# Block sums of the output weights: a table of their own over slots 25 to 56, laid back by DMA, and a new order of the steady batches

## The chip, the cores and the metric

One core of a Trainium2 chip runs the whole program. The metric is device time in microseconds (us); lower is better. Engine names are those of the profile: PE (TensorE matmul), PEld (TensorE weight loads), DVE (VectorE), ACT (ScalarE), POOL (GpSimd), SP (SyncE, which here issues nearly all DMAs).

## What is computed

The reference, cut to what matters: an attention over 32 learned memories, then a feed-forward layer with a hard-swish gate, all in fp32.

```python
# q, k, v: (8, 8, 576, 64)   phi: (8, 8, 576, 32)   w_in: (512, 2048)   w_out: (2048, 512)
a = softmax(phi, over the 32 memories)
k_m, v_m = einsum('bhsm,bhsd->bhmd', a, k), einsum('bhsm,bhsd->bhmd', a, v)
attn = softmax(q @ k_m.T / 8)
x = (attn @ v_m), heads side by side: (8 * 576, 512)
h = x @ w_in
out = (h * clip(h + 3, 0, 6) / 6) @ w_out
```

## The kernel before

**Tiling.** A batch has 576 tokens: two halves of 256 and 320 (the last 64 of a batch are a rest, joined in pairs over two batches). `v_m` is folded into `w_in` for each batch (`fold`, L424), so that the first product (`gemm1`) runs over 256 probabilities instead of 512 features. The 2048 hidden features are 16 tiles of 128. An fp32 product is made of three fp32r products: each operand is split into a rounded high part and the difference, the low part.

**First stages: slots.** Batches 0 to 2 run through 56 slots. A slot is one tile of 128 features for a whole batch: `g` (`gemm1`, 12 matmuls, L487), `u` (relu on ACT, L497), `m` (gate on DVE, L503), `k` (rest tokens, ACT), `h` (high part on ACT, L516), `l` (low part on DVE, L521), and two slots later (`LAG`) `a` (`gemm2`, L541). `BEGIN` is a hand-written order of slots 0 to 39 with the preparation of the weights and of the attention; `THIRD` is a table of what else is put into slots 40 to 55 (batch 2). From slot 8 on, one PSUM tile `ph` serves all slots, so the next `gemm1` must wait until the gate of the slot before has read it.

**Steady batches: units.** Batches 3 to 7 run in 32 steps each. Two steps make a unit, two tiles of 128 features, and the second product of a unit is done with Strassen's seven block products instead of eight (`products`, L685). It needs sums and differences of the four 256-column blocks of `w_out`: four blocks stay in `w2_sb` (two of them replaced by differences) and three sums per unit of weights are kept in DRAM (`streams`) and fetched again for each use (`stream<-kept`). `FOURTH`, `STEADY` and `EVERY` are the tables of what else is done in which step: `xa` and `xe` (subtract the maximum, exponential of phi), `mem` (the `pk` matmuls, L319), `sc` and `ct` (scores, L357, and their transposition on DVE, L373), `fo`, `vh`, `vl` (fold of `w_in` and its split), `fetch` (a chunk of `w_in` back from DRAM), `kv`, `pt`, `pn` (loads).

**The block sums before.** `tw` adds the high and low part of a unit's weights to whole fp32 numbers (POOL, L639), `ts` makes the three sums (POOL, L644, L645), `th` splits them (ACT L648, DVE L649, through `halve`) and stores them, `td` makes the two differences (POOL, L660) and `dd` splits these into `w2_sb` (ACT, DVE). Units 6, 7, 5, 0, 1, 2 and 3 are done in `THIRD`, 4 in `FOURTH`, and the differences of 5, 6 and 7 in steps 6 to 15 of batch 3 (`tl`, POOL L668, L670). Each engine runs its instructions in the written order.

Of the kernel before, what the change touches and what calls it, by code (L numbers as in the profile page):

```python
# [10 lines left out]
F32 = mybir.dt.float32  # L11
F32R = mybir.dt.float32r
# [9 lines left out]
P = 128  # L22
# [16 lines left out]
TMP = {"tag": "tmp", "bufs": 3}  # L39
# [69 lines left out]
5 xa.N.0 / 6 xe.N.0 xa.N.1 / 7 xe.N.1 xa.N.2 / 8 xe.N.2 mem.N / 9 nr.N nk.N q.N.0 pn.M / 10 q.N.1 / 11 tp.N tk.N  # L109
/ 12 sc.N.0 ct.N.0 / 13 cm.N.0 pt.M / 14 cs.N.0 sc.N.1 ct.N.1 fetch.N.0 / 15 cm.N.1 ex.N.0 kv.M.0 / 16 cs.N.1 ds.N.0 dr.N.0 kv.M.1  # L110
/ 17 ex.N.1 dm.N.0 kv.M.2 fetch.N.1
/ 20 fo.N.0 vh.N.0.0 vl.N.0.0 / 21 vh.N.0.1 vl.N.0.1 fetch.N.2 / 22 ds.N.1 dr.N.1 mx.M.0 kv.M.3 / 23 bt.N.0 dm.N.1
/ 24 fo.N.1 vh.N.1.0 vl.N.1.0 bh.N.0 / 25 vh.N.1.1 vl.N.1.1 bl.N.0 fetch.N.3 / 26 mx.M.1 kv.M.4 / 27 bt.N.1 mt.M mo.M
/ 28 fo.N.2 vh.N.2.0 vl.N.2.0 / 29 vh.N.2.1 vl.N.2.1 sp.M
"""


@with_exitstack
def attention_ffn_kernel(ctx: ExitStack, tc: tile.TileContext, pn, pt, kv, kl, qt, w1, w2, out):
# [16 lines left out]
    places, turns = {}, [0]  # L136
# [494 lines left out]
    def blocks_(u, half):
        return w2_sb[u][:, half].rearrange("p (x c) -> p x c", c=VC)

    def blocks(u, half):
        return blocks_(u, half).bitcast(F32)

    def sum_whole(u):
        staged[u] = sb.tile([P, 4, VC], F32, name="whole", **TMP)
        nc.gpsimd.tensor_tensor(staged[u], blocks(u, 0), blocks(u, 1), ALU.add)  # L639

    def sum_streams(u):
        w = staged[u]
        s_ = staged[u, "s"] = sb.tile([P, 3, VC], F32, name="sums", **O_RING)
        nc.gpsimd.tensor_tensor(s_[:, 1:3], w[:, 0:2], w[:, 2:4], ALU.add)  # L644
        nc.gpsimd.tensor_tensor(s_[:, 0], w[:, 0], w[:, 3], ALU.add)  # L645
# [5 lines left out]
    def keep_streams(u, k):  # L651
        xs = ((1, 2), (0,))[k]
        t = sb.tile([P, len(xs), 2, VC], F32R, name="parts", **TMP)
        halve(t[:, :, 0], t[:, :, 1], staged[u, "s"][:, xs[0] : xs[-1] + 1])
        for k, x in enumerate(xs):
            nc.sync.dma_start(out=streams[u][x], in_=t[:, k].bitcast(F32))

    def difference(u):
        w = staged[u]
        nc.gpsimd.tensor_tensor(w[:, 1:3], w[:, 1:3], w[:, 0::3], ALU.subtract)  # L660

    def late_difference(u, k):
        if k == 0:
            staged[u] = sb.tile([P, 4, VC], F32, name="whole", **O_RING)
        d = staged[u]
        if k < 2:
            part = blocks(u, k)
            nc.gpsimd.tensor_tensor(d[:, 0::3] if k else d[:, 1:3], part[:, 1:3], part[:, 0::3], ALU.subtract)  # L668
        else:
            nc.gpsimd.tensor_tensor(d[:, 1:3], d[:, 1:3], d[:, 0::3], ALU.add)  # L670
# [18 lines left out]
    BLOCK = {"A22": 0, "M7": 1, "M6": 2, "M1": 3, "M5": 4, "M2": 5, "A11": 6}  # L689

    def rounded_pair(low_ring):
        high = xpool.tile([P, 7, P], F32R, name="high", tag="probs00") if low_ring[0] % 2 == 0 else None
        if high is None:
            high = sb.tile([P, 7, P], F32R, name="high", **TMP)
        low_ring[0] += 1
        return high, sb.tile([P, 7, P], F32R, name="low", **TMP)

    ring = [0]

    class Unit:  # L700
# [61 lines left out]
        def products(self, part):  # L762
# [11 lines left out]
            todo = {
                0: (("A11", 0, 1, kept(2)), ("M5", 0, 0, kept(3)), ("M2", 1, 0, kept(0))),
                1: (("A22", 2, 0, kept(1)), ("M6", 3, 1, part and stream(1)), ("M7", 3, 0, part and stream(2)),
                    ("M1", 2, 1, part and stream(0))),
            }[part]
# [6 lines left out]
        def leave_first(self):  # L785
# [3 lines left out]
            nc.scalar.mul(self.x[:, 3], m[1][:, :VC], 1.0 / 6.0)  # L789

        def leave_second(self):
            m, x = sums[self.b, self.half], self.x
            o = sb.tile([P, 4, VC], F32, name="o", **O_RING)
            nc.scalar.mul(x[:, 1], m[2][:, :VC], 1.0 / 6.0)
            m1 = m[2][:, VC:].unsqueeze(1).broadcast_to([P, 2, VC])
# [3 lines left out]
            self.o = o  # L799
# [13 lines left out]
    class RestUnit:  # L813
# [4 lines left out]
        def total(self):  # L818
            own = {0: ("probs10", wpool), 2: ("probs00", xpool)}.get(self.u)
# [292 lines left out]
```

## Time and profile before

| | us |
|---|---|
| median of 3 runs (lowest, highest) | 723.74 (723.48, 724.48) |
| the profiled execution, its own time | 723.54 |
| its span in the trace | 721.8 |
| PE busy (weight loads apart) | 690.0, 96% of the span |
| DVE, ACT, POOL busy | 558.3, 387.1, 323.8 |

The span is what the rows below are counted in; 1.7 us of the execution lie outside it. A busy PE is not PE at its peak, since matmuls are pipelined and a matmul's length is longer than the distance to the next. Slots and units are found in the trace by their `gemm1`: slot 25 begins at 138.01, slot 40 at 202.62, the first unit at 293.11, its second `gemm1` at 302.48, the last step of batch 7 ends shortly after 702.

### The profile page before, as it was taken

Reading aid. Unit: us, or ns where it says so; the run is one execution under the profiler, and the core shown is the slowest. Engines: PE = TensorE matmul, PEld = TensorE weight load, DVE = VectorE, ACT = ScalarE, POOL = GpSimd, SP = SyncE. Lnnn points to the kernel's source line nnn. Section 1 sums busy time; section 2 is a strip of 40 time slices with the busy share of each in tenths; the row PEclk is TensorE's granted clock in tenths of the full one; section 3 lists DMA queues with packets and bytes.
Section 4 is the critical chain, followed back from the end, with each engine's and each line's share of the span. In section 5 each row is a group of like instructions: output and inputs, shape, how many; then the busy total and the mean of one; then the engine's idle time right before and its main releaser. Section 6 shows DMA issues by size and latency. Waiting matters only on the chain.

```text
span 721.8 us, 14655 instructions
## 1 busy us (share of the span) xinstructions
PE 690.0 (96%) x5618; PEld 584.5 (81%) x5622; DVE 558.3 (77%) x986; ACT 387.1 (54%) x786; POOL 323.8 (45%) x315
## 2 busy tenths in 40 slices
PE   8999999999999989799999999999999999999997
PEld 4456777888787766588889898888989989889997
DVE  4899986766366776688998779886898768977765
ACT  4677776544344445354655455554555546555553
POOL 1645331521227555358645345452646336444434
PEclk9999999999999999899999999999999999999999
DMA  9987671737143833569782398836983466736351
GB/s 360 416 332 272 227 276 57 273 112 250 51 149 125 316 154 110 175 223 343 257 308 77 103 349 298 308 119 223 345 308 114 132 231 214 277 107 210 133 182 45
DMA packets 56413, 154.46 MB, mean 214 GB/s; under 512 B 6168, under 2 KB 7192, under 8 KB 51736
## 3 DMA queue, kind: packets, MB, share of 16 engines
q1 hardware_dynamic: 56264, 153.47, 60.0%
q8 instruction: 44, 0.72, 0.4%
q14 instruction: 25, 0.20, 0.1%
q10 hardware_dynamic: 80, 0.07, 0.0%
HBM read 131.48 MB, written 22.03 MB: 213 GB/s over the span
## 4 chain that ended last, share of the span: by engine, by line
PE 67%; DVE 17%; ACT 6%; DMA 3%; issue 3%; POOL 2%; SPq 0%; ACTq 0%; DVEq 0%; POOLq 0%
PE acc L685 25%; PE acc L541 14%; PE ph L715 13%; PE ph L487 8%; PE pv L424 4%; DVE low L760 3%; DVE parts L649 2%; DMA stream<-kept 2%; PE acc L873 2%; DVE gf L503 2%; DVE gated L734 1%; DVE glo L521 1%; ACT high L755 1%; DVE gated L744 1%; DVE pnat L305 1%
## 5 line engine op out<-in xcount | busy, mean ns | idle before, releaser
L748 POOL TENSOR_TENSOR gated<-gated 128x256 f32<-128x256 f32 x80 | 77.3, 967 | 201.4 <-DVE gated L734 178.1
L760 DVE TENSOR_TENSOR low<-gated,high 128x384 fp32r<-128x384 f32 (+1 forms) x160 | 136.6, 855 | 27.4 <-ACT high L755 25.3
L715 PE MATMUL ph<-probs,both 128*128 128x256 f32 (+1 forms) x960 | 152.5, 294 | 1.7 <-DVE gf L503 1.7
L755 ACT CAST high<-gated 128x384 fp32r<-128x384 f32 (+1 forms) x160 | 90.6, 568 | 87.8 <-DVE gated L744 79.9
L715 PEld LDWEIGHTS ph<-probs,both 128*128 128x128 f32 x960 | 133.0, 188 | 2.5 <-DVE gf L503 2.2
L685 PE MATMUL acc<-w,high 128*128 128x256 f32 x640 | 123.9, 286 | 0.6 <-ACT high L755 0.3
L721 ACT ACTIVATE gf<-ph,three 128x256 f32<-128x256 f32 (+1 forms) x160 | 80.1, 500 | 64.5 <-PE ph L715 63.9
L685 PEld LDWEIGHTS acc<-w,high 128*128 128x128 f32 x640 | 99.4, 188 | 18.8 <-issue 6.3
L541 PE MATMUL acc<-w,ghi 128*128 128x512 f32 x384 | 101.9, 401 | 0.0
L734 DVE SCALAR_TENSOR_TENSOR gated<-gf,ph 128x256 f32<-128x256 f32 x160 | 65.7, 410 | 38.3 <-ACT gf L721 38.0
L685 PE MATMUL acc<-w,low 128*128 128x256 f32 x320 | 90.7, 283 | 2.2 <-DVE low L760 2.0
L685 PE MATMUL acc<-stream,high 128*128 128x256 f32 x480 | 89.1, 281 | 1.7 <-DMA stream<-kept 1.6
L541 PEld LDWEIGHTS acc<-w,ghi 128*128 128x128 f32 x384 | 70.1, 191 | 25.2 <-issue 5.7
L487 PEld LDWEIGHTS ph<-probs,both 128*128 128x128 f32 x528 | 74.0, 188 | 18.3 <-DVE gf L503 13.4
L487 PE MATMUL ph<-probs,both 128*128 128x256 f32 (+1 forms) x528 | 78.1, 297 | 8.3 <-DVE gf L503 8.2
L685 PEld LDWEIGHTS acc<-stream,high 128*128 128x128 f32 x480 | 73.3, 188 | 2.8 <-DMA stream<-kept 2.8
L685 PE MATMUL acc<-stream,low 128*128 128x256 f32 x240 | 67.2, 280 | 0.0
L685 PEld LDWEIGHTS acc<-w,low 128*128 128x128 f32 x320 | 60.2, 188 | 4.0 <-DVE low L760 3.8
L497 ACT ACTIVATE gf<-ph,three 128x576 f32<-128x576 f32 (+2 forms) x52 | 36.6, 705 | 43.4 <-PE ph L487 37.4
L503 DVE SCALAR_TENSOR_TENSOR gf<-gf,ph 128x576 f32<-128x576 f32 x44 | 32.9, 748 | 30.0 <-ACT gf L497 29.9
L541 PE MATMUL acc<-w,glo 128*128 128x512 f32 x192 | 53.8, 389 | 0.0
L444 DVE TENSOR_TENSOR both<-pv,both 128x512 fp32r<-128x512 f32 x62 | 42.3, 683 | 14.5 <-ACT both L435 14.3
(116 smaller groups left out, 1117.0 us busy)
## 6 DMA issues: line engine op xcount, KB each, us to landing
stream<-kept SPq DMA_DIRECT2D x186, 256.0 KB, 3.8
w<-w_kept SPq DMA_DIRECT2D x24, 1024.0 KB, 7.3
kvt<-in_kv SPq DMA_DIRECT2D x32, 516.0 KB, 6.7
raw<-in_w SPq DMA_DIRECT2D x16, 512.0 KB, 7.6
raw<-in_w SPq DMA_DIRECT2D x8, 1024.0 KB, 12.2
out_t<-o SPq DMA_DIRECT2D x16, 512.0 KB, 3.1
kept<-parts SPq DMA_DIRECT2D x24, 256.0 KB, 2.2
pnat<-in_pn SPq DMA_DIRECT2D x8, 576.0 KB, 7.2
```

The source lines that it names most:

```text
L444: nc.vector.tensor_tensor(both[:, 1], src, both[:, 0].bitcast(F32), ALU.subtract)
L487: nc.tensor.matmul(dst, w[:, g, fs], x[:, g * n : (g + 1) * n], start=(i == 0), stop=(i == len(seq) - 1),)
L497: nc.scalar.activation(self.gf, self.h, AF.Relu, bias=three)
L503: nc.vector.scalar_tensor_tensor(self.gf, relu, 6.0, self.h, ALU.min, ALU.mult)
L541: nc.tensor.matmul(accs[self.b, self.rest, k].rearrange("p (x c) -> p x c", c=VC), left[:, t * P : (t + 1) * P], w, start=k in self.first ...
L685: nc.tensor.matmul(dst, left[l], right[r], start=begin and n == 0, stop=end and n == 2, skip_group_check=True)
L715: nc.tensor.matmul(h, w[:, g, fs], x[:, g * self.n : (g + 1) * self.n], start=(i == 0), stop=(i == len(seq) - 1))
L721: nc.scalar.activation(self.gf, self.h[k], AF.Relu, bias=three)
L734: nc.vector.scalar_tensor_tensor(dst, by_tile(self.gf), 6.0, by_tile(self.h[k]), ALU.min, ALU.mult)
L748: nc.gpsimd.tensor_tensor(g[:, 2:4], g[:, 0::8], g[:, 1:8:6], ALU.subtract)
L755: nc.scalar.copy(self.parts[0][:, at], self.g[:, 1:8][:, at])
L760: nc.vector.tensor_tensor(low[:, at], self.g[:, 1:8][:, at], high[:, at].bitcast(F32), ALU.subtract)
```

## The change

The block sums get their own table, `CONVERT`: unit u begins in slot 25 + 4u and takes five slots (`tw`, `ts`, `th.u.0`, then `to2.u.0` with `th.u.1`, then `to2.u.1`). The low parts of sums and differences are subtracted on POOL instead of DVE. The differences go through DRAM: `to2` stores them (`placed`), `rp` loads them over the two blocks of `w2_sb` in slots 44, 46, ... 54 and in steps 0 and 3 of batch 3. The work tiles are a ring of three of their own (`tmp0` to `tmp2`, in the pool whose tiles all begin at multiples of 256 bytes), which later holds the units' high and low parts too. `THIRD` loses the conversion words and has its attention words in an earlier order; `EVERY` is rewritten, with each `fetch` in two halves. The block products M1, M2 and A22 change columns within their PSUM banks.

```diff
-0 fold.C.1 un.C.1.0 un.C.1.1 exps.N.0 tw.6 / 1 exps.N.1 exps.N.2 ts.6 tw.7 / 2 mem.N th.6.0 th.6.1 ts.7 tw.5
...
+0 fold.C.1 un.C.1.0 un.C.1.1 exps.N.0 / 1 exps.N.1 exps.N.2 / 2 mem.N / 3 norm.N / 4 turn.N / 5 score.N.0 centre.N.0
...
-5 xa.N.0 / 6 xe.N.0 xa.N.1 / 7 xe.N.1 xa.N.2 / 8 xe.N.2 mem.N / 9 nr.N nk.N q.N.0 pn.M / 10 q.N.1 / 11 tp.N tk.N
...
+0 sp.N / 5 fetch.N.0.0 / 6 xa.N.0 / 7 xe.N.0 fetch.N.0.1 / 8 xa.N.1 xa.N.2 / 9 xe.N.1 fetch.N.1.0 / 10 xe.N.2 / 11 mem.N fetch.N.1.1
...
+CONVERT = (25, 29, 33, 37, 41, 45, 49, 53)
...
+    def stage(u, k):
+        return wpool.tile([P, 4, VC], F32R, name="stage", tag=f"tmp{(2 * u + k) % 3}")
...
+    def sum_blocks(u):
+        w = staged[u].bitcast(F32)
+        staged[u, "s"] = stage(u, 1)
+        s_ = staged[u, "s"].bitcast(F32)
+        nc.gpsimd.tensor_tensor(s_[:, 0:2], w[:, 0:2], w[:, 2:4], ALU.add)
+        nc.gpsimd.tensor_tensor(w[:, 1:3], w[:, 1:3], w[:, 0::3], ALU.subtract)
+        nc.gpsimd.tensor_tensor(w[:, 0], w[:, 0], w[:, 3], ALU.add)
 
     def halve(high, low, whole_):
         nc.scalar.copy(high, whole_)
-        nc.vector.tensor_tensor(low, whole_, high.bitcast(F32), ALU.subtract)
...
+        nc.gpsimd.tensor_tensor(low, whole_, high.bitcast(F32), ALU.subtract)
...
     def replace(u):
-        high, low = (blocks_(u, k)[:, 1:3] for k in range(2))
-        halve(high, low, staged[u][:, 1:3])
+        nc.sync.dma_start(out=w2_sb[u][:, :, VC : 3 * VC].bitcast(F32), in_=placed[u])
...
+        convert = {}
+        for u, at in enumerate(CONVERT):
+            for k, words_ in enumerate(("tw.{0}", "ts.{0}", "th.{0}.0", "to2.{0}.0 th.{0}.1", "to2.{0}.1")):
+                convert.setdefault(at + k, []).extend(words_.format(u).split())
```

What this moves, engine by engine. First DVE at the end of batch 2, slots 53 to 55 (`glo` is a slot's low part, `gf` its gate, `both` the split of a fold, `parts` and `w_3_811` the low parts of the block sums). Before:

```order
L503 SCALAR_TENSOR_TENSOR gf<-gf,ph_574 128x576
L444 TENSOR_TENSOR both<-pv,both 128x512 x2
L521 TENSOR_TENSOR glo<-gf,ghi 128x512
L503 SCALAR_TENSOR_TENSOR gf<-gf,ph_574 128x576
L649 TENSOR_TENSOR w_3_811<-whole,w_3_811 128x512
L649 TENSOR_TENSOR parts<-sums,parts 128x2x256
L649 TENSOR_TENSOR parts<-sums,parts 128x256
L521 TENSOR_TENSOR glo<-gf,ghi 128x512
L503 SCALAR_TENSOR_TENSOR gf<-gf,ph_574 128x576
```

And in the changed kernel, the same place:

```order
L504 SCALAR_TENSOR_TENSOR gf<-gf,ph_582 128x576
L445 TENSOR_TENSOR both<-pv,both 128x512 x2
L522 TENSOR_TENSOR glo<-gf,ghi 128x512
L504 SCALAR_TENSOR_TENSOR gf<-gf,ph_582 128x576
L522 TENSOR_TENSOR glo<-gf,ghi 128x512
L504 SCALAR_TENSOR_TENSOR gf<-gf,ph_582 128x576
```

The three L649 instructions that stood between a gate and the next low part are gone from DVE's queue. Next POOL of the changed kernel in slots 24 to 29, where the first conversion stands (`stage` is the new work tile; L639 `tw`, L645 to L647 `ts`, L651 the low parts; `st` are attention scores, L202 is a split of other weights):

```order
L202 TENSOR_TENSOR w_6_1550<-tmp,w_6_1550 128x1024
L639 TENSOR_TENSOR stage<-w_0_497 128x1024
L388 TENSOR_TENSOR st<-st,mx 128x640
L645 TENSOR_TENSOR stage<-stage 128x512
L646 TENSOR_TENSOR stage<-stage 128x512
L647 TENSOR_TENSOR stage<-stage 128x256
L651 TENSOR_TENSOR stage<-stage 128x512
L651 TENSOR_TENSOR stage<-stage 128x256
L400 TENSOR_TENSOR st<-st,sm 128x512
L651 TENSOR_TENSOR stage<-stage 128x512
L639 TENSOR_TENSOR stage<-w_1_701 128x1024
```

Before, these rows of POOL held only the L202 and `st` instructions (there L203, L387, L399). Last ACT around the exponentials of phi in the first half of a steady batch (`pnat` is phi, whose third exponential `pk` waits for; L721 a step's relu, L755 the high parts). Before:

```order
L309 ACTIVATE pnat<-pnat 128x512
L721 ACTIVATE gf<-ph_2927,three 128x256
L309 ACTIVATE pnat<-pnat 128x512
L755 CAST high<-gated 128x384
L721 ACTIVATE gf<-ph_2926,three 128x256
L755 CAST high<-gated 128x512
L309 ACTIVATE pnat<-pnat 128x128
L721 ACTIVATE gf<-ph_2927,three 128x256
L336 ACTIVATE kvn<-pk,rs 128x128 x2
```

And now (L310, L718 and L752 are the same operations):

```order
L310 ACTIVATE pnat<-pnat 128x512
L752 CAST rounded<-gated 128x384
L718 ACTIVATE gf<-ph_2959,three 128x256
L752 CAST rounded<-gated 128x512
L310 ACTIVATE pnat<-pnat 128x128
L718 ACTIVATE gf<-ph_2960,three 128x256
L752 CAST rounded<-gated 128x384
L718 ACTIVATE gf<-ph_2959,three 128x256
L752 CAST rounded<-gated 128x512
L337 ACTIVATE kvn<-pk,rs 128x128 x2
```

The last exponential now stands one step ahead of the step whose `pk` matmuls read it (step 10 and `mem` in step 11; both were in step 8).

## Rows read from the trace of the kernel before

**Rows 1.** Windows: stretch, its length, busy PE, PEld, DVE, ACT, POOL, clock, DMA.

```profile
138.01:202.62 64.61, 64.61 (x373) 53.63 (x372) 37.69 (x55) 27.04 (x51) 17.01 (x9) 1.00 0.46 168
202.62:302.48 99.86, 89.72 (x613) 69.01 (x612) 67.14 (x87) 43.90 (x92) 51.20 (x34) 0.95 0.47 168
302.48:702.00 399.52, 389.08 (x3535) 359.11 (x3534) 327.53 (x648) 216.22 (x458) 197.13 (x225) 1.00 0.64 219
508.89:547.53 38.64, 38.15 (x314) 34.52 (x313) 34.65 (x76) 21.98 (x44) 19.79 (x22) 1.00 0.87 310
```

**Rows 2.** Waits of PE, 202.62 to 302.48: total us, times, longest.

```profile
PE ph L487 <- DVE gf L503: 6.0, 4, 2.2
PE pv L424 <- issue: 2.4, 1, 2.4
PE ph L715 <- DVE gf L503: 1.7, 1, 1.7
```

**Rows 3.** Timeline, all engines, 275 to 285: start, length, engine, instruction.

```profile
275.33 3.22 DVE L649 TENSOR_TENSOR parts<-sums,parts 128x512 fp32r<-128x512 f32 x2
275.49 2.78 POOL L639 TENSOR_TENSOR whole<-w 128x1024 f32<-128x1024 f32 x1 [1.90 <-DVE w L649]
...
278.48 1.76 DVE L521 TENSOR_TENSOR glo<-gf,ghi 128x512 fp32r<-128x512 f32 x1
...
280.16 0.74 DVE L503 SCALAR_TENSOR_TENSOR gf<-gf,ph 128x576 f32<-128x576 f32 x1
...
280.96 1.85 PE L487 MATMUL ph<-probs,both 128*128 128x320 f32 x12 [1.75 <-DVE gf L503]
...
284.17 0.68 DVE L521 TENSOR_TENSOR glo<-gf,ghi 128x512 fp32r<-128x512 f32 x1
```

**Rows 4.** Timeline of PE, 262 to 302.

```profile
262.01 2.02 PE L487 MATMUL ph<-probs,both 128*128 128x320 f32 x12 [2.23 <-DVE gf L503]
263.96 1.96 PE L424 MATMUL pv<-w,kvT 64*32 64x512 f32 x16
...
275.17 1.09 PE L424 MATMUL pv<-w,kvT 64*32 64x512 f32 x16
276.19 2.11 PE L541 MATMUL acc<-w,ghi 128*128 128x512 f32 x8
...
296.51 1.96 PE L424 MATMUL pv<-w,kvT 64*32 64x512 f32 x16 [2.43 <-issue]
298.41 3.32 PE L541 MATMUL acc<-w,ghi 128*128 128x512 f32 x8
```

**Rows 5.** Groups by line and form: busy us, mean ns of one.

```profile
L649 DVE TENSOR_TENSOR parts<-sums,parts 128x256 fp32r<-128x256 f32 x8 | 15.4, 1931 | 0.0
L649 DVE TENSOR_TENSOR w<-whole,w 128x512 fp32r<-128x512 f32 x8 | 7.4, 926 | 6.4 <-ACT w L648 6.3
L649 DVE TENSOR_TENSOR parts<-sums,parts 128x512 fp32r<-128x512 f32 x8 | 6.3, 786 | 4.6 <-ACT parts L648 4.6
L639 POOL TENSOR_TENSOR whole<-w 128x1024 f32<-128x1024 f32 x8 | 21.8, 2719 | 16.1 <-DVE w L649 15.9
L413 POOL TENSOR_TENSOR probs<-pT,probs 128x512 fp32r<-128x512 f32 x7 | 11.2, 1599 | 0.0
L373 DVE STREAM_TRANSPOSE st<-psc 128x640 f32<-128x640 f32 x7 | 5.8, 831 | 0.4 <-POOL w L203 0.4
```

**Rows 6.** Waits of PE, 302.48 to 722.

```profile
PE pk L319 <- ACT pnat L309: 4.3, 5, 1.0
...
PE acc L685 <- DMA stream<-kept: 1.6, 3, 0.9
PE psc L357 <- DVE st L373: 1.6, 1, 1.6
```

**Rows 7.** Wait of POOL, 202.62 to 302.48.

```profile
POOL sums L644 <- DMA out_t<-o: 29.0, 2, 20.2
```

**Rows 8.** DMA issues: KB each, us to landing.

```profile
kept<-parts SPq DMA_DIRECT2D x24, 256.0 KB, 2.2
```

More of the change, by code (lines that the diff above doesn't have):

```diff
@@ L135, in attention_ffn_kernel @@
     w1_sb, w2_sb, raw = {}, {}, {}
-    places, turns = {}, [0]
+    places, turns = {}, [0, 0]
     def vw_tag(b=0, r=0):
@@ L628, in attention_ffn_kernel @@
     streams = [[dram.tile([P, 2, VC], F32, name=f"kept{u}_{x}") for x in range(3)] for u in range(NFT // 2)]
+    placed = [dram.tile([P, 2, 2 * VC], F32, name=f"placed{u}") for u in range(NFT // 2)]
     staged, streamed = {}, {}
[L631 to L635, printed above, removed]
+    def stage(u, k):
+        return wpool.tile([P, 4, VC], F32R, name="stage", tag=f"tmp{(2 * u + k) % 3}")
@@ L637, in sum_whole @@
     def sum_whole(u):
[L638 to L645, printed above, removed]
+        w = staged[u] = stage(u, 0)
+        parts = [w2_sb[u][:, k].bitcast(F32).rearrange("p (x c) -> p x c", c=VC) for k in range(2)]
@@ L651, in keep_streams, with halve_blocks @@
[L651 to L658, printed above, removed]
+        nc.gpsimd.tensor_tensor(low, whole_, high.bitcast(F32), ALU.subtract)
+    def halve_blocks(u, k):
         w = staged[u]
-        nc.gpsimd.tensor_tensor(w[:, 1:3], w[:, 1:3], w[:, 0::3], ALU.subtract)
@@ L662, in late_difference @@
-    def late_difference(u, k):
         if k == 0:
[L664 to L668, printed above, removed]
-        else:
-            nc.gpsimd.tensor_tensor(d[:, 1:3], d[:, 1:3], d[:, 0::3], ALU.add)
+            s_, t = staged[u, "s"], stage(u, 2)
+            staged[u, "t"] = t
+            halve(t[:, 0:2], t[:, 2:4], s_[:, 0:2].bitcast(F32))
@@ L772, in stream @@
                 return [streamed[u][x][:, k] for k in range(2)]
[L774 to L778, printed above, removed]
+            todo = (
+                (("A11", 0, 1, kept(2)), ("M5", 0, 0, kept(3)), ("M2", 1, 1, kept(0))),
+                (("A22", 2, 1, kept(1)), ("M6", 3, 1, part and stream(1)), ("M7", 3, 0, part and stream(2)),
+                 ("M1", 2, 0, part and stream(0))),
+            )[part]
             begun = set()
@@ L818, in total @@
         def total(self):
-            own = {0: ("probs10", wpool), 2: ("probs00", xpool)}.get(self.u)
-            self.parts = (own[1] if own else sb).tile([P, 6, P], F32R, name="parts", **({"tag": own[0]} if own else TMP))
+            self.parts = rounded(6, SPARE[self.u])
             self.pair = rest[:, 2 * self.u : 2 * self.u + 2]
@@ L989, in attention_ffn_kernel @@
                 order = list(range(NFT // 2))[:: -1 if half else 1]
-                units += [Unit(b, half, u, k == 0, k == len(order) - 1) for k, u in enumerate(order)]
+                units += [Unit(b, half, u, len(units) + k) for k, u in enumerate(order)]
         def half_step(i, between=None):
```

99 lines of the change are left out of this document (59 added, 40 removed).

## The prediction

> **What bounds the kernel now.** I went from the page's shares to the stretches, then to the waits of the engine that is nearly always busy, then to the timeline at those waits. The page has PE busy for 96% of the span, so time is won only where PE idles or runs slowly. The stretches [rows 1] say where that is. In slots 25 to 39 PE is busy for all of 64.61 us. From slot 40 to the second step of the units it is busy for 89.72 of 99.86 us, which leaves 10.1 idle, and the granted clock is 0.95 there against 1.00 elsewhere. The steady batches leave 399.52 - 389.08 = 10.4 us idle in four times the length.
>
> Who is late in the second stretch? The waits of PE name DVE's gate `gf` for 6.0 + 1.7 us in five waits, and one wait of 2.4 us before a fold that shows no releaser [rows 2]. The timeline shows what holds the gate back [rows 3]. At 275.33 DVE begins the two low parts of a conversion and needs 3.22 us for both, beside a POOL addition of 2.78 us. Then the slot's own low part takes 1.76 us, where an undisturbed one takes 0.68, and the next gate comes so late that PE idles 1.75 us before its `gemm1` at 280.96. That these are waits and not work can be read from the groups: the 256-wide `parts` take 1931 ns on average and the 512-wide 786, so the narrower one is slower [rows 5]. A DVE instruction that reads two SBUF tiles stands still while POOL works on one.
>
> The clock loss hangs on the same idling [rows 4]. After 2.23 us idle, the fold at 263.96 takes 1.96 us, where the same 16 matmuls take 1.09 at 275.17: 0.87 lost. After 1.73 and 2.43 us idle [rows 2], the fold at 296.51 takes 1.96 again and the eight matmuls behind it 3.32 instead of 2.11: 2.08 lost. That is 1.2 GHz in place of 2.4 for a few us, some 2.9 us in all.
>
> **Third segment: conversions off DVE.** Removed from DVE's queue are 24 instructions, 15.4 + 7.4 + 6.3 = 29.1 us [rows 5], nearly all of them in the stretch where DVE is busy for 67.1 of 99.9 us. Behind them stood `glo` and the gate, and behind the gate PE and ACT (ACT's copy of the rest tokens waits for it too). What can be won is the idle 10.1 plus the clock's 2.9, 13.0 us; the least is nothing, if another wait takes its place. I take 11.5. I leave 1.5, since POOL still runs its 2.7 us additions and a `glo` can still stand behind one; but with a gate of 0.74 and a `glo` of 0.68 [rows 3] as the only regular DVE work of a slot (4.3 us: 64.61 over the 15 slots 25 to 39), one such wait fits.
>
> **POOL's new work.** Two 512-wide and one 256-wide low part per conversion: 16 at 1.6 us, and 8 at half of that, from the like subtraction of L413 [rows 5], make 32 us more; the differences of units 5 to 7, which POOL made in steps 6 to 15, become cheaper by some us and are not counted. POOL is busy for 51.2 of 99.9 us in the third segment and for 17.0 of 64.6 before it [rows 1], and half of all conversions now fall into that emptier stretch. So POOL has room, and I cost its work at nothing by itself.
>
> **Slots 25 to 39.** PE has no idle time there to give and four conversions are new. DVE is busy for 37.7 of 64.6 us [rows 1], so it has 27 us of its own to lose. How much lateness does a slot forgive? At 275 to 281 DVE was late by at least 3.22 - 2 x 0.79 = 1.6 us in `parts` and 1.76 - 0.68 = 1.1 in `glo`, 2.7 together, and PE idled 1.75 [rows 3, 5]: about 1 us was forgiven. So the cost is 0 below, and above one POOL addition of 2.7 us per conversion less that 1 us: 4 x 1.7 = 6.8 us. I take +0.5, near the lower end, because here one instruction can be caught in a slot and not two in a row.
>
> Here a rule speaks against the change. The Trainium skill (SBUF — State Buffer, Who interferes with whom) says that VectorE and GpSimd share one port pair under an exclusive lock: a VectorE instruction with two SBUF inputs and a GpSimd one that reads SBUF exclude each other for their whole length. The timeline agrees (0.68 and 1.76 us for the same `glo`). By that rule every us that moves to POOL is again a us in which DVE can be shut out, and moving the low parts removes the victim only in part; the second rival below is that case.
>
> **Laying back by DMA.** ACT and DVE no longer write the differences; eight stores and eight loads do, on SP's queue, which also carries the loads of `w_in`, of the next batch and of the streams. A load `rp` waits for the stored copy and for the last `gemm2` that reads the blocks, and everything behind it on SP waits too. The nearest row is the store of a sum, 2.2 us to landing [rows 8]; a slot is 4.3, and `rp` stands 19 slots (unit 0) down to 7 (unit 6) after the slot in which its conversion begins. I take 0; the upper end is a rival. POOL's waits for a transfer, 29.0 us in two because the sums shared a ring with the outputs [rows 7], go with that ring; they stopped only conversions, so no gain is booked.
>
> **Addresses and columns.** The block tiles' new addresses could change how fast engines or DMAs read them; the trace names no address, so no row shows it. In the steady stretch a matmul costs 389.08 / 3535 = 0.110 us of PE [rows 1]; a pace better or worse by 1% would be 3.9 us. I take 0, since nothing in the rows singles these tiles out, and keep 3.9 either way for the range.
>
> **Steady batches.** PE waits 4.3 us in five places for the exponential of phi before `pk` and 1.6 for the transposed scores before the second `psc` [rows 6]. In the new table the exponential stands a step ahead of `pk`, and the two score products are four steps apart instead of two; both waits should go. The 1.6 us for streams stay, since the same MB are fetched, now in halves. The order is denser at the end of a batch: the sums over scores, both transpositions back and three folds stand in steps 22 to 30. I take -5.5; the bounds are -9 (nearly all of the idle 10.4) and +7 (third rival).
>
> **Sum.** -11.5 + 0.5 + 0 - 5.5 = -16.5. The profiled execution took 723.5 us by its own time (721.8 in the trace and 1.7 around it), 0.2 below the median of 723.7. So 723.5 - 16.5 = 707.0.
>
> **Rivals.** First, all of it goes: 13.0 and 9 us, 723.5 - 22 = 701.5. For it speaks that the waits have one cause; against it, that some `glo` will stand behind POOL.
>
> Second, the port stays the trouble. Half of the third segment's waits remain (-6), the early slots pay 3 and the steady table gives 4: 723.5 - 6 + 3 - 4 = 716.5. For it speaks `glo` at 1.76 us behind a POOL sum, in a place where no conversion stood on DVE directly before; against it, that PE's waits came only where three DVE instructions stood between two gates.
>
> Third, DVE fills up in second halves. In the second half of batch 5 it is busy for 34.65 of 38.64 us [rows 1]; two reductions and two transpositions of the scores, four instructions of at most 0.83 us [rows 5], move into this half, and the score matmuls that lengthen it move with them. If all of it comes on the path in four batches, 4 x 3 = 12 us go against the gain of 5.5: 707 + 12 = 719. It decides if DVE falls more than about a step behind; PE's waits for DVE there were small so far, which speaks against it.
>
> Fourth, the other side: the three work tiles are still being stored when POOL wants them. `ts` of the next unit writes over a tile whose stores SP issued one slot before. POOL then stands, ACT's rounding stands behind POOL, and the relu of the next slot behind ACT: PE pays eight times. Stores land in 2.2 us [rows 8], within the slot. With stores 5 us late and 1 forgiven it is 8 x 4 = 32 us: 707 + 32 = 739. It decides at about 16.5 / 8 + 1 = 3.1 us. For it speaks POOL's long waits for a transfer [rows 7]; against it the 2.2.
>
> Fifth, the stalls have another cause and PE waits elsewhere for as long: 723 to 724.
>
> **How the numbers follow.** Chances: forecast 0.58, first rival 0.09, second 0.15, third 0.07, fourth 0.07, fifth 0.04. The predicted time is 707, its own range 702 to 712. Leaving out the fourth and fifth, a part of the first and the outer edge of the second and third leaves 698 to 719. Faster by over 0.2% (1.4 us, about what a measurement of this kernel can tell from none) holds in the first four cases but for a few of their worst ends: 0.87; within 0.2%: 0.04; slower: 0.09.
>
> **What would show it.** Right: in the stretch between slot 40 and the units, no wait of PE for `gf` over 1 us, clock 1.00 throughout, and some 87 to 89 us instead of 99.9; DVE with no instruction of the conversions; `pk` waits gone from PE's list. Wrong: new waits of PE in slots 25 to 39 (its 64.61 us would grow), POOL waiting for `kept` or `placed` stores, SP standing at `rp` while a fold or a stream waits, or waits of the second halves' matmuls for DVE.

## The result, and the profile after

The changed kernel takes 711.95 us (710.93 to 714.79, four runs) against 723.61 us of the kernel before in the same comparison (723.09 to 724.48): ratio 0.984, 95% interval 0.981 to 0.988. It is faster, and inside the stated range of 702 to 712 by 0.05 us, but 5 us above the 707.0 that was predicted. The profiled execution was the slowest of the four, with 714.79 us and a span of 712.7; one stretch below shows where it lost time that other profiles did not.

The stretches that answer to [rows 1] (slots 25 to 39; slot 40 to the second `gemm1` of the units; from there to the last step):

```profile
137.76:203.56 65.80, 65.29 (x374) 53.54 (x373) 39.42 (x53) 31.02 (x59) 49.65 (x34) 1.00 0.62 225
203.56:293.13 89.57, 86.35 (x614) 69.19 (x612) 47.23 (x67) 42.51 (x87) 47.75 (x38) 0.98 0.59 208
293.13:690.17 397.04, 392.14 (x3519) 363.07 (x3518) 318.02 (x643) 215.62 (x455) 177.96 (x217) 1.00 0.66 226
```

For the kernel before, the third stretch cut at the same step is this:

```profile
302.48:700.02 397.54, 387.11 (x3520) 357.12 (x3519) 326.39 (x645) 215.69 (x457) 197.13 (x225) 1.00 0.64 219
```

So slots 25 to 39 cost 65.80 - 64.61 = 1.2 us, and the third segment gained 99.86 - 89.57 = 10.3, DVE having 47.23 us of work there instead of 67.14. In the steady batches, where 5.5 us were expected, 0.5 came. Yet PE's idle time there fell from 10.4 (397.54 - 387.11) to 4.9 us, by just the 5.5 (a coincidence, as the part on the prediction shows). The same matmuls (x3520 and x3519) took PE 5.0 us longer. That is the whole puzzle of this result. The rest of the span is small: -0.2 us before slot 25 and +0.8 after the last step.

PE's waits, first from slot 40 to the units (answers to [rows 2]), then in the steady batches (answers to [rows 6]): total us, times, longest.

```profile
PE pk L320 <- ACT pnat L310: 1.6, 2, 1.2
PE pv L425 <- PE ph L488: 0.7, 1, 0.7
PE ph L488 <- DVE gf L504: 0.5, 1, 0.5
...
PE acc L685 <- DVE rounded L757: 2.1, 6, 0.5
PE pv L425 <- DMA w<-w_kept: 1.9, 1, 1.9
PE acc L685 <- DMA stream<-kept: 1.0, 3, 0.4
```

The waits for the gate are 0.5 us in place of 7.7. Before the steady `pk` and `psc` there are none left. New is one wait of a fold for a chunk of `w_in`. What a slot looks like now (timeline, answers to [rows 3]):

```profile
273.41 1.51 POOL L651 TENSOR_TENSOR stage<-stage 128x512 fp32r<-128x512 f32 x1 [0.73 <-ACT stage L650]
...
275.14 0.75 DVE L504 SCALAR_TENSOR_TENSOR gf<-gf,ph 128x576 f32<-128x576 f32 x1 [1.36 <-ACT gf L498]
275.28 2.11 PE L542 MATMUL acc<-w,ghi 128*128 128x512 f32 x8
...
278.13 1.72 PE L488 MATMUL ph<-probs,both 128*128 128x320 f32 x12
...
279.16 0.68 DVE L522 TENSOR_TENSOR glo<-gf,ghi 128x512 fp32r<-128x512 f32 x1
...
280.72 0.76 DVE L504 SCALAR_TENSOR_TENSOR gf<-gf,ph 128x576 f32<-128x576 f32 x1 [0.88 <-ACT gf L498]
```

The gate at 275.14 is done 2.2 us before the `gemm1` at 278.13 that needs it; the gate now waits for ACT's relu, and PE no longer for the gate.

**What is left of the port.** In slot 42 the same collision happens once more, with other work:

```profile
216.11 1.60 POOL L645 TENSOR_TENSOR stage<-stage 128x512 f32<-128x512 f32 x1
216.51 2.70 DVE L303 TENSOR_TENSOR pnat<-pnat,nmxb 64x128 f32<-64x128 f32 x2
...
217.79 1.27 POOL L646 TENSOR_TENSOR stage<-stage 128x512 f32<-128x512 f32 x1
...
219.24 0.31 ACT L310 ACTIVATE pnat<-pnat 128x128 f32<-128x128 f32 x1 [1.99 <-DVE pnat L303]
219.60 0.46 PE L320 MATMUL pk<-kvt,pnat 64*32 64x129 f32 x16 [1.22 <-ACT pnat L310]
219.99 3.61 PE L542 MATMUL acc<-w,ghi 128*128 128x512 f32 x8
```

Two subtractions with a quarter of `glo`'s columns take 1.35 us each, and the second ends just after POOL's second sum does. (In e2, where POOL stands still as they begin, the same two took 0.58 us together.) PE idles 1.22 us, and the eight matmuls behind it take 3.61 instead of 2.11: the clock has gone to its lower level, with a granted clock of 0.58 from 219.6 to 223.6. In seven later kernels that leave this place as it is (e1, e3 to e7, e10) PE idles 1.2 us there too, but the clock stayed up, and the segment took 88.1 to 88.6 us. So the clock's 1.5 us belong to this one execution.

**What the laying back costs.** POOL's groups and one of its waits, slots 25 to 55 (answers to [rows 5] and [rows 7]), and the stores (answers to [rows 8]):

```profile
L651 POOL TENSOR_TENSOR stage<-stage 128x512 fp32r<-128x512 f32 x16 | 21.8, 1362 | 28.0 <-ACT stage L650 28.0
L651 POOL TENSOR_TENSOR stage<-stage 128x256 fp32r<-128x256 f32 x8 | 6.3, 789 | 0.0
...
POOL stage L639 <- DMA kept<-stage: 12.9, 2, 8.4
...
kept<-stage SPq DMA_DIRECT2D x24, 256.0 KB, 4.4
placed<-stage SPq DMA_DIRECT2D x16, 256.0 KB, 6.6
```

POOL's new work is 28 us, near the 32 estimated. Its stores land in 4.4 and 6.6 us (medians), not in 2.2, and POOL does wait for them up to 8.4 us; but PE's idle time in slots 25 to 39 is 0.5 us in all, and no wait in its list after them names a store.

**The new fold wait.** The chain of waits around the first step of batch 5, and the fold before it: start, us, what.

```profile
447.13 1.02 PE pv L425 x16
448.14 1.63 PE acc L685 x12
...
451.79 6.67 DMA w<-w_kept
458.46 0.14 issue
458.60 1.50 PE pv L425 x16
460.10 2.74 PE acc L685 x12
```

`fetch.N.3.1`, the second half of the last chunk, stands in step 29 behind three loads of streams on SP's queue. It is issued at 451.79, 4.1 us before the `gemm1` of step 0 (455.86), and lands 6.67 us later; the fold that reads it is in step 0. PE idles 1.87 us, then runs at the lower clock (0.60 granted from 458.6 to 462.8): the fold takes 1.50 us and the twelve block products behind it 2.74, where the fold at 447.13 and its twelve took 1.02 and 1.63. That the clock falls is no fixed part of it: e6 and e7 idle 2.0 and 2.1 us at this fold and lose the clock too, e1 idles 2.3 and keeps it.

### The profile page after: what moved, and what is told of

Same layout as the page of the kernel before. It is cut to its first block, busy times and chain, and to the rows that moved or that the text cites. A ratio compares the mean times of both kernels' runs of the same rounds, so it can differ in the third digit from the quotient of the medians.

```text
span 712.7 us, 14748 instructions
## 1 busy us (share of the span) xinstructions
PE 692.2 (97%) x5618; PEld 590.5 (83%) x5622; DVE 531.6 (75%) x962; ACT 389.4 (55%) x786; POOL 332.9 (47%) x333
## 4 chain that ended last, share of the span: by engine, by line
PE 61%; DVE 10%; DMA 9%; POOL 6%; ACT 4%; issue 2%; SPq 0%; POOLq 0%; ACTq 0%; DVEq 0%
PE acc L685 30%; PE ph L712 15%; PE acc L542 6%; PE ph L488 4%; PE pv L425 3%; DMA stream<-kept 2%; PE pk L320 2%; DMA kept<-stage 1%; DMA kvt<-in_kl 1%; POOL stage L639 1%; DVE gf L504 1%; POOL tmp L191 1%; DMA out_t<-o 1%; POOL w L202 1%; DMA w<-w_kept 1%
## 5 line engine op out<-in xcount | busy, mean ns | idle before, releaser
L685 PE MATMUL acc<-w,rounded 128*128 128x256 f32 x1248 | 182.0, 287 | 2.3 <-DVE rounded L757 2.1
L685 PEld LDWEIGHTS acc<-w,rounded 128*128 128x128 f32 x1248 | 162.9, 190 | 23.3 <-ACT rounded L752 9.4
L757 DVE TENSOR_TENSOR rounded<-gated,rounded 128x384 fp32r<-128x384 f32 (+1 forms) x160 | 133.6, 835 | 37.6 <-ACT rounded L752 31.1
L752 ACT CAST rounded<-gated 128x384 fp32r<-128x384 f32 (+1 forms) x160 | 90.4, 566 | 86.9 <-DVE gated L741 80.9
L718 ACT ACTIVATE gf<-ph,three 128x256 f32<-128x256 f32 (+1 forms) x160 | 80.0, 500 | 61.9 <-PE ph L712 61.0
L685 PE MATMUL acc<-stream,rounded 128*128 128x256 f32 x720 | 102.0, 285 | 1.0 <-DMA stream<-kept 1.0
L685 PEld LDWEIGHTS acc<-stream,rounded 128*128 128x128 f32 x720 | 93.3, 193 | 2.9 <-DMA stream<-kept 2.9
L488 PEld LDWEIGHTS ph<-probs,both 128*128 128x128 f32 x528 | 74.2, 188 | 11.7 <-DVE gf L504 6.3
L522 DVE TENSOR_TENSOR glo<-gf,ghi 128x512 fp32r<-128x512 f32 x44 | 37.2, 848 | 13.2 <-ACT ghi L517 11.8
L436 ACT CAST both<-pv 128x512 fp32r<-128x512 f32 x62 | 36.1, 584 | 17.5 <-DVE both L445 8.8
L542 PEld LDWEIGHTS acc<-w,glo 128*128 128x128 f32 x192 | 36.3, 189 | 8.1 <-DVE glo L522 0.3
```

Of the source, the lines that this page charges most:

```text
L488: nc.tensor.matmul(dst, w[:, g, fs], x[:, g * n : (g + 1) * n], start=(i == 0), stop=(i == len(seq) - 1),)
L522: nc.vector.tensor_tensor(self.glo[:, :n], self.gated(), self.ghi[:, :n].bitcast(F32), ALU.subtract)
L542: nc.tensor.matmul(accs[self.b, self.rest, k].rearrange("p (x c) -> p x c", c=VC), left[:, t * P : (t + 1) * P], w, start=k in self.first ...
L685: nc.tensor.matmul(dst, left[l], right[r], start=begin and n == 0, stop=end and n == 2, skip_group_check=True)
L718: nc.scalar.activation(self.gf, self.h[k], AF.Relu, bias=three)
L757: nc.vector.tensor_tensor(low[:, at], self.g[:, 1:8][:, at], high[:, at].bitcast(F32), ALU.subtract)
```

## Experiments

Two theories for the lost 5 us in the steady batches: the new addresses of the block tiles slow the block products down (the address), or the rewritten table pays back what it gains, by a denser order or a late transfer (the table). And two for the third segment: taking the low parts off DVE is what helps (the engine), or spreading the conversions is (the spreading, with what came along: the ring, the DMA, the new order of `THIRD`). The letters in the quoted expectations are each expectation's own. Eleven kernels, each timed beside the kernel before (723.0 to 723.4 us in these comparisons). The runs of one kernel spread by 1 to 4 us, so the medians alone do not tell two kernels apart whose intervals overlap. "Steady" is the stretch from the second `gemm1` of the units to the last step, in the profiled execution; "distance" is the mean distance from one block product's start to the next, gaps over 200 ns left out, worked out from the trace's start times.

| | median us | ratio, 95% interval | steady us, PE busy | distance ns |
|---|---|---|---|---|
| before | 723.4 | 1 | 397.54, 387.11 | 117.4 |
| after | 711.95 | 0.984 (0.981 to 0.988) | 397.04, 392.14 | 120.1 |
| e1, tiles at 64 | 707.73 | 0.978 (0.976 to 0.980) | 390.62, 384.33 | 115.7 |
| e2, low parts on DVE | 715.02 | 0.989 (0.987 to 0.990) | | 120.1 |
| e3, old table | 711.71 | 0.983 (0.982 to 0.985) | 397.48, 390.65 | 120.0 |
| e4, earlier fetch | 708.59 | 0.979 (0.978 to 0.981) | 392.42, 389.65 | 120.1 |
| e5, e1 and e4 together | 702.63 | 0.971 (0.968 to 0.974) | 386.88, 383.32 | 116.2 |
| e6, tiles at 128 | 711.09 | 0.983 (0.980 to 0.985) | 393.66, 390.01 | 118.5 |
| e7, tiles at 32 | 710.42 | 0.981 (0.978 to 0.984) | 394.67, 389.48 | 118.4 |
| e8, before with tiles at 256 | 727.53 | 1.006 (1.004 to 1.007) | 400.64, 391.48 | 120.1 |
| e9, before with low parts on POOL | 718.55 | 0.994 (0.993 to 0.996) | | 117.4 |
| e10, e5 with the old columns | 703.24 | 0.973 (0.971 to 0.975) | 387.15, 383.60 | 116.0 |
| e11, e5 with an earlier exponential | 701.48 | 0.971 (0.969 to 0.973) | | 115.9 |

**e1, the block tiles 64 bytes past a multiple of 256.** The tiles come from the other pool, whose tiles begin there.

```diff
-        return wpool.tile([P, 4, VC], F32R, name="stage", tag=f"tmp{(2 * u + k) % 3}")
+        return xpool.tile([P, 4, VC], F32R, name="stage", tag=f"tmp{(2 * u + k) % 3}")
...
-        return (xpool if tag == "probs00" else wpool).tile([P, n, P], F32R, name="rounded", tag=tag)
+        return xpool.tile([P, n, P], F32R, name="rounded", tag=tag)
```

> The changed kernel, with the ring tmp0 to tmp2 and probs10 moved into the pool whose tiles begin at 64 bytes past a multiple of 256; nothing else. Theory A (the address sets the pace): the distance between block products (L685) falls from 120 ns to about 117, 1968 of them, so some 5.5 us less than the changed kernel: about 706. Rival B (the pace is that of the new columns or of the denser table): distance stays at 120 ns, time stays at 711 to 713.

It took 707.73 us, 4.2 less than the changed kernel, so the address theory holds, with a smaller gain than forecast. The groups of the block products of this kernel, then of the changed one (busy us and mean ns behind the first bar):

```profile
L685 PE MATMUL acc<-w,rounded 128*128 128x256 f32 x1248 | 178.4, 283 | 3.4 <-DVE rounded L757 3.1 <-ACT rounded L752 0.4
L685 PE MATMUL acc<-stream,rounded 128*128 128x256 f32 x720 | 98.8, 281 | 1.0 <-DMA stream<-kept 0.9
```

```profile
L685 PE MATMUL acc<-w,rounded 128*128 128x256 f32 x1248 | 182.0, 287 | 2.3 <-DVE rounded L757 2.1
L685 PE MATMUL acc<-stream,rounded 128*128 128x256 f32 x720 | 102.0, 285 | 1.0 <-DMA stream<-kept 1.0
```

Each of the 1968 products is some 4 ns shorter, 6.8 us of busy time, of which a part is the lower clock behind the fold, which the profile of e1 does not have: against e4, whose profile does not have it either, the gain is 4.8 us (282.0 - 277.2); 1.0 us comes back as waits for DVE's low parts (2.1 to 3.1), which PE now reaches sooner. The old table (e3) and the earlier fetch (e4) leave the distance at 120, so it does not come from the table.

**e2, the low parts of the conversions on DVE again,** everything else as changed.

```diff
-        nc.gpsimd.tensor_tensor(low, whole_, high.bitcast(F32), ALU.subtract)
+        nc.vector.tensor_tensor(low, whole_, high.bitcast(F32), ALU.subtract)
```

> The changed kernel, with the low parts of the conversions subtracted on VectorE again; they stay spread over slots 25 to 56 and are still laid back by DMA. Theory A (three instructions of VectorE between two gates make PE wait): half of the eight conversions lie in slots 40 to 56, so PE waits for gf come back there, 1 to 2 us for each of four, and a few in slots 25 to 39: 4 to 8 us more than the changed kernel, 716 to 720. Rival C (the gain came from spreading the conversions and from their own ring): no more than 1.5 us slower, 711 to 714.

715.02 us, 3.1 more than the changed kernel and between the two forecasts. On balance all of it is lost in slots 25 to 39; the third segment is as long as in the kernels whose clock stayed up there (windows of e2, slots 25 to 39 and slot 40 to the units, and PE's waits for the gate in each):

```profile
138.03:208.48 70.45, 67.40 (x373) 54.72 (x372) 45.99 (x64) 32.23 (x62) 40.02 (x25) 0.98 0.58 211
208.48:296.66 88.18, 84.66 (x613) 67.99 (x612) 51.73 (x81) 41.11 (x84) 31.84 (x22) 1.00 0.62 217
PE ph L488 <- DVE gf L504: 3.0, 2, 2.4
PE ph L488 <- DVE gf L504: 3.1, 2, 1.7
```

So the forecast waits for the gate do come back, two in each stretch. In the third segment their 3.1 us stand in place of the waits for `pk` (1.6) and for a fold (0.7), which e2 does not have. There, the rest of the change without the engine takes the waits for the gate from 7.7 us to 3.1 and the segment from 99.86 to 88.18; whether this is the spreading itself, the ring, the DMA or the new order of `THIRD`, no run parts. The change of engine takes the waits for the gate on to 0.5 and keeps the early slots cheap (65.80 instead of 70.45).

**e3, the steady batches' old table,** with whole chunks fetched as in the kernel before, and the spreading of phi's maxima for batch 4 (`spread`) put into slot 53, which the old table expects there.

```diff
-/ 20 sc.N.1 ct.N.1 pn.M / 21 cm.N.0 cs.N.0 cm.N.1 kv.M.1 / 22 fo.N.0 vh.N.0.0 vl.N.0.0 / 23 fetch.N.2.0 vh.N.0.1 vl.N.0.1 ex.N.0 cs.N.1 fetch.N.2.1
...
+/ 12 sc.N.0 ct.N.0 / 13 cm.N.0 pt.M / 14 cs.N.0 sc.N.1 ct.N.1 fetch.N.0 / 15 cm.N.1 ex.N.0 kv.M.0 / 16 cs.N.1 ds.N.0 dr.N.0 kv.M.1
```

> The changed kernel with the steady batches' table of before (and the spread of the maxima for batch 4 back in slot 53). Theory A (the new table gains, and the pace hides it): the waits of pk for the exponential and of psc for the transposed scores come back, 5 to 6 us, less the 2 to 3.5 us that the late half of the w_in chunk costs in batch 5: 2 to 4 us slower than the changed kernel, 714 to 717. Rival D (the new table gives nothing): within 1 us.

711.71 us, equal to the changed kernel, where the first theory had 714 to 717: as a whole the rewritten table gained nothing. The waits show what it is the balance of. With the old table `pk` waits again, and no fold waits for a chunk (waits of PE, steady batches of e3). PE's idle time is 6.8 us even so, 3.6 less than before:

```profile
PE pk L320 <- ACT pnat L310: 3.3, 4, 1.0
PE acc L685 <- DMA stream<-kept: 1.3, 2, 0.8
```

**e4, the late half fetched three steps earlier.**

```diff
-/ 24 ... / 26 vh.N.1.1 vl.N.1.1 mx.M.1 fetch.N.3.0
+/ 24 ... / 26 vh.N.1.1 vl.N.1.1 mx.M.1 fetch.N.3.0 fetch.N.3.1
...
-... / 29 vh.N.2.1 vl.N.2.1 bl.N.0 fetch.N.3.1
+... / 29 vh.N.2.1 vl.N.2.1 bl.N.0
```

> The changed kernel with the second half of the last w_in chunk of a batch fetched in step 26 instead of 29. Theory A: the wait of the fold at the start of batch 5 (1.94 us idle, and half the clock behind it, 3.5 us together against the step of before) is gone, so up to 3.5 us less than the changed kernel's profiled run and 0 to 2 us less in the median: 709 to 712, with less spread from run to run. Rival E (the transfer is late because the memory is busy, whenever it is issued): the wait stays or moves to a stream, no difference.

708.59 us, 3.4 less and just under the forecast. The wait for the chunk is gone, nothing takes its place, and the window of the steady batches falls to 392.42 us. All of PE's waits there over 0.3 us:

```profile
PE acc L685 <- DVE rounded L757: 2.0, 6, 0.4
PE acc L685 <- DMA stream<-kept: 0.8, 2, 0.4
```

Against e3, the table is now worth 711.7 - 708.6 = 3.1 us.

**e5, both repairs.** The edits of e1 and e4 together.

> The changed kernel with both repairs at once: block tiles 64 bytes past a multiple of 256, and the second half of the last w_in chunk fetched in step 26 instead of 29. Theory (two separate costs, one of pace and one of a late transfer, which add): 712 - 4.2 - 3.4 = 704.4, so 703 to 706; the fold waits under 0.5 us for the chunk, and the block products start about 116 ns apart. Rival (both repairs took away the same loss, for instance the fall of the clock behind the fold): 707 to 708.5, no better than either alone.

702.63 us, 9.3 less than the changed kernel, and no less than the 4.2 + 3.4 of the two alone: they are separate costs. The 1.7 us beyond the sum are within the spread of the runs. The steady window of e5:

```profile
292.19:679.07 386.88, 383.32 (x3520) 354.13 (x3519) 316.91 (x643) 214.69 (x455) 177.83 (x217) 1.00 0.68 232
```

**e6 and e7, other addresses.** As e1, with the first tile of the pool (64 bytes in e1) twice and half as long, which shifts the block tiles to 128 and to 32 bytes past a multiple of 256. The other tiles of this pool, the probabilities of the first halves among them, and those of `sb` move by the same bytes. The edit of e6:

```diff
-        threes = xpool.tile([P, M // 2], F32, name="three")
+        threes = xpool.tile([P, M], F32, name="three")
```

> The changed kernel with the block tiles at 128 bytes past a multiple of 256, in place of 0. Theory A1 (what counts is the start modulo 128 bytes): as the changed kernel, 711 to 713, block products about 120 ns apart. Theory A2 (what counts is the start modulo 256): between or as with 64 bytes, 707 to 709, about 116 ns apart. Rival B (not the address, but something that the 64-byte version shifted by chance): anything, without a change of the distance between block products.

> The changed kernel with the block tiles at 32 bytes past a multiple of 256. Theory A (only a start at a multiple of 256 or 128 is slow): 707 to 709, block products about 116 ns apart, as with 64 bytes. Rival (64 bytes is what helps, and 32 bytes is as bad as 0): 711 to 713, about 120 ns apart.

711.09 and 710.42 us: 0.9 and 1.5 under the changed kernel, which the times cannot tell from none, but with distances of 118.5 and 118.4 ns, between 120.1 and 115.7. Neither theory's form of a rule (modulo 128, modulo 256, only 0 is slow) comes out: 64 is the best of four, 0 the worst, 32 and 128 lie between. The distance changes with the address each time, so a shift by chance, without a change of the distance, falls as an explanation; the rule stays open.

**e8, the kernel before, with its work tiles moved to multiples of 256.** Nothing else.

```diff
-        return high, sb.tile([P, 7, P], F32R, name="low", **TMP)
+        return high, wpool.tile([P, 7, P], F32R, name="low", **TMP)
```

> The kernel before, whose ring of work tiles and whose tile probs00 are put at multiples of 256 bytes; nothing else is changed. Theory A (the address sets the pace of the block products): they start about 120 ns apart instead of 117, over some 1970 of them 5 to 6 us, so 727.5 to 730. Rival (the pace comes from the rewritten table, the denser DMAs or the new columns, not from the address): within 1 us of the kernel before, 722.5 to 724.5.

727.53 us against 723.01, ratio 1.006 (1.004 to 1.007): 4.5 us slower. In the old order and the old columns the distance goes from 117.4 to 120.1 ns, and PE's busy time in the steady batches from 387.11 to 391.48 (window of e8):

```profile
302.23:702.87 400.64, 391.48 (x3520) 362.34 (x3518) 326.34 (x646) 215.74 (x457) 196.98 (x225) 1.00 0.63 218
```

Nothing but addresses differs here, and they cost what the changed kernel lost.

**e9, the kernel before, with only the low parts moved to POOL.** The conversions stay packed into slots 40 to 55.

```diff
-        nc.vector.tensor_tensor(low, whole_, high.bitcast(F32), ALU.subtract)
+        nc.gpsimd.tensor_tensor(low, whole_, high.bitcast(F32), ALU.subtract)
```

> The kernel before, with only the low parts of the block sums subtracted on POOL instead of DVE; the conversions stay where they were, in slots 40 to 55. Theory (it is the DVE instructions between two gates that hold PE up, so that taking them off DVE's queue is enough): the third segment loses 6 to 10 of its 10 us of idle time, 713 to 718. Rival (what cures it is the spreading: with the conversions as dense as before, POOL falls behind, ACT's rounding stands behind POOL and the relu behind ACT): within 2 us of the kernel before, 721 to 725, and PE's waits name the gate or the relu again.

718.55 us, 4.6 less than before, just outside the first theory's figures. The third segment takes 93.02 us, 6.8 less, as that theory said, but DVE is not all of it. The rival's relay is there too, once (timeline of e9):

```profile
235.56 1.28 POOL L660 TENSOR_TENSOR whole<-whole 128x512 f32<-128x512 f32 x1
...
236.88 0.62 ACT L648 CAST w<-whole 128x512 fp32r<-128x512 f32 x1 [4.76 <-POOL whole L660]
237.41 0.92 ACT L648 CAST parts<-sums 128x512 fp32r<-128x512 f32 x2
...
238.23 0.73 ACT L497 ACTIVATE gf<-ph,three 128x576 f32<-128x576 f32 x1
...
238.99 0.76 DVE L503 SCALAR_TENSOR_TENSOR gf<-gf,ph 128x576 f32<-128x576 f32 x1 [5.93 <-ACT gf L497]
...
239.80 2.61 PE L487 MATMUL ph<-probs,both 128*128 128x320 f32 x9 [2.21 <-DVE gf L503]
```

ACT stands 4.76 us at a rounding that waits for POOL, the relu behind it is late, so is the gate, and PE idles 2.21 us. Both theories hold in part: in the third segment the engine alone gets 6.8 us and the change without the engine 11.7 (e2), and the engine matters most where a conversion is put into slots that had none.

**e10, the old columns of M1, M2 and A22 in e5.**

```diff
-                (("A11", 0, 1, kept(2)), ("M5", 0, 0, kept(3)), ("M2", 1, 1, kept(0))),
...
+                (("A11", 0, 1, kept(2)), ("M5", 0, 0, kept(3)), ("M2", 1, 0, kept(0))),
...
```

> The version with both repairs (702.6), with the block products M1, M2 and A22 back in the columns of the kernel before. Theory (the columns cost and bring nothing): 702 to 703.5, block products 116 ns apart. Rival (the new columns are part of why the block products are now closer together than the 117 to 118 ns of the kernel before at the same addresses): 704.5 to 706.5.

703.24 us, a steady window of 387.15 against 386.88 and a distance of 116.0 ns against 116.2: no cost and no gain of the columns can be seen. (The kernel before did not have its tiles at the addresses of e5, as the rival takes it; see the end of the next part.)

**e11, the exponential of slot 41 a slot earlier, in e5.**

```diff
-0 fold.C.1 un.C.1.0 un.C.1.1 exps.N.0 / 1 exps.N.1 exps.N.2 / 2 mem.N
+0 fold.C.1 un.C.1.0 un.C.1.1 exps.N.0 exps.N.2 / 1 exps.N.1 / 2 mem.N
```

> The version with both repairs (702.6), with the last third of batch 3's exponential of phi moved from slot 41 to 40, before the conversion of unit 4 reaches POOL. Theory (the wait for pk in slot 42 comes from the two 64x128 subtractions that stand behind POOL's sums, 1.6 us and a half clock behind it): 700 to 701.5, and the pk wait is gone from PE's list. Rival (the 512-wide subtraction then stands behind POOL alone and pk is as late): 702 to 703.5, the wait stays.

701.48 us, with the same ratio as e5 (0.971), so no gain can be told from the times. In the trace the wait shrinks from 1.6 to 0.5 us, so the place named was right; the third segment is 87.1 us long instead of 88.3:

```profile
PE pk L320 <- ACT pnat L310: 0.5, 1, 0.5
```

## Why the prediction was right, and where not

**Third segment, -11.5: right in size, half right in cause.** It gained 10.3 in the profiled execution with its lower clock in slot 42, 11.2 to 11.8 in the seven kernels without it. The length stated, 87 to 89 us, was met by those seven and missed by 0.6 in the profile of the changed kernel. The allowance of 1.5 us for one more collision behind POOL was met by the `pk` in slot 42. The reason given, conversions off DVE, was only a part: alone it gives 6.8 us (e9), and without it the rest of the change shortens the segment as much (e2), though the waits for the gate are then 3.1 us and not 0.5.

**Slots 25 to 39, +0.5: mis-sized, 1.2,** inside the bounds. Of it 0.5 is idle and 0.7 busier PE. e2 comes near the upper bound of 6.8: with DVE's low parts kept, the four conversions cost 5.8 us. What moved to POOL did not shut DVE out as the second rival had it; one case of it is left, the two small subtractions of slot 42 with 1.35 us each. The Trainium skill's exclusive port (SBUF — State Buffer, Who interferes with whom) agrees with this case.

**Laying back, 0: right, for a reason that was not the one given.** Stores do not land within the slot: 4.4 and 6.6 us, beyond the 3.1 from which the fourth rival was to decide. POOL waited, 12.9 us in two waits, and PE did not, so the rival's eight payments do not follow from a late store. That a spread order leaves ACT's rounding time to wait is the likely reason, not a shown one. Where POOL is packed, the relay from POOL over ACT and the gate costs PE 2.21 us (e9).

**Addresses, 0 ± 3.9: the term that failed.** "I take 0, since nothing in the rows singles these tiles out" should have been a price: it measured 4.5 us in the kernel before (e8) and 4.2 back in the changed one (e1), beyond the 3.9 kept for it; PE's busy time grew by 5.0 us, some 1.6 of them at the lower clock behind the fold of batch 5. No row of before could show the sign, but its block tiles stood elsewhere, and the diff moved nearly all of them to one kind of address. The columns, costed with it, were worth nothing (e10).

**Steady batches, -5.5: the waits went, but not all by the table, and a new one came.** The waits for `pk` and `psc` went as forecast. Two of them, 2.6 us, stand in batch 3 of the kernel before (PE's waits from 302.48 to 380.5):

```profile
PE psc L357 <- DVE st L373: 1.6, 1, 1.6
PE pk L319 <- ACT pnat L309: 1.0, 1, 1.0
```

e3 has neither of them, with the old table: they went when the conversions left batch 3. What was said of the fetches, "the same MB are fetched, now in halves", missed that the last half is issued four steps later than the old whole chunk and that a fold stands behind it: 1.87 us idle and the clock, 3.4 us in the times (e4). Without it the table gives 3.1 us in the times (e4 against e3) and 5.1 us in the profiles (392.42 against 397.48).

**The sum.** With the address at 4.2, the late half at 3.4 and slots 25 to 39 at 0.7 more, 707.0 becomes 715.3, which is 3.3 above the 711.95 measured. So something was also better than costed. Without the late half PE's idle time in the steady batches falls from 10.4 to 2.8 us (e4), by 7.7 where 5.5 were taken, which makes 2.2 of the 3.3; that it fell by just 5.5 with it is luck. Of the 7.7, 3.6 are there with the old table (e3). Most of these lie in batch 3, whose steps 0 to 15 no longer hold late differences and the conversion of unit 4: it takes 75.35 us in e3, but 78.24 in e8, which has the same table of steady batches, the same kind of addresses, and the old conversions. In their windows PE's idle time makes 2.4 of these 2.9 us:

```profile
292.41:367.76 75.35, 74.54 (x681) 67.09 (x680) 61.47 (x128) 41.03 (x85) 32.24 (x39) 1.00 0.87 310
```

```profile
302.23:380.47 78.24, 75.03 (x680) 67.18 (x679) 68.69 (x128) 42.34 (x87) 45.68 (x46) 1.00 0.78 270
```

The prediction said of the late differences that they were not counted. No rival came as it was told; the result lies between the forecast and the second rival, by other mechanisms. That it lies inside the range is luck: two costs taken at nothing, 7.6 us together, were partly made up by gains that were not costed.

**Open.** Which rule of the address sets the pace. What was moved is the operand loaded as weights: the block tiles give the 128 columns that PEld loads, while the 256-wide operand, `w2_sb` or a stream, stayed in the pool of multiples of 256 in every kernel; its own offset was not tried. In the kernel before, as it is laid out, a third of the block products of its units read their tile 64 bytes past a multiple of 256 and the others 224 past. Nor is it shown that the slowed matmul's own operand is what counts. The 256-wide matmuls of the steady `gemm1`, whose two operands keep their offsets from before to after, e1 and e8, go along with the block products: mean distances of 116.7, 118.4, 115.9 and 118.5 ns. That other engines' accesses to the moved tiles slow PE's reads is a rival that no run rules out. The profiles and the times of the changed kernel differ by 2.8 us, of which the clock in slot 42 accounts for 1.5.

## What to carry to other kernels

When a diff moves operands of a kernel that TensorE bounds, treat their addresses as an edit of its own: compare the distance between matmuls before and after, and try two or three offsets before judging the rest. A transfer that is split in halves is as late as its second half: look for the fold or product that reads it, and count the steps to it. Before a side job is moved to an emptier engine, see whether a change of its place in time does the same: here the engine alone gained 6.8 us in the dense stretch and the rest of the change without it 11.7, and the engine mattered most where the job was newly put.

## What the hardware showed that was not expected

The start address of the block tiles changes the pace of the same 128x256 matmuls, by a way that is open: mean distances of 120.0 to 120.1 ns at multiples of 256 bytes, 118.5 at 128 past them, 118.4 at 32, and 115.7 to 116.2 at 64, some 4 us of 712 between the best and the worst. The Trainium skill (SBUF — State Buffer, Operand start alignment) says which starts are legal, and that its runs timed nothing; these runs do. About the same idle time of PE did not always cost the clock: 1.2 us before `pk` lowered it in one profile and not in seven others. And a store of 256 KB out of the work tiles takes 4.4 us to land where the same bytes took 2.2 [rows 8]: in two of the three stores of a unit the halves lie apart in the tile now, and other transfers run beside them, which no run here separates.
